# Retention attention and a SwiGLU block on one core: six instead of five pieces of a tick's vector work behind each plain down step

## The chip, the cores and the metric

The kernel runs on one core of a Trainium2 chip. The metric is the device time of one execution in microseconds (us); shorter is better. Engines are named as the profile names them: PE (matrix products), PEld (its weight loads), DVE (vector), ACT (scalar), POOL, and SP, which issues most of the transfers. Each engine runs its own instructions in the order in which they stand; semaphores tie them together.

## The reference

Attention with a decay in place of the softmax, for 8 batches x 8 heads x 576 positions x 64 columns, and behind it a SwiGLU block over 4608 tokens of 512 columns with 1536 hidden columns. All is float32.

```python
scores = scale * np.matmul(q, k.transpose(0, 1, 3, 2))
gamma = 1.0 - 2.0 ** (-5.0 - np.arange(H, dtype=np.float32))
Dmat = np.where(rel >= 0, gamma[:, None, None] ** rel[None, :, :], 0.0)   # rel = i - j
attn_out = np.matmul(scores * Dmat[None, :, :, :], v)
x = attn_out.transpose(0, 2, 1, 3).reshape(B * S, H * D)
g = x @ w_gate
silu = g * (1.0 / (1.0 + np.exp(-g)))
out = (silu * (x @ w_val) @ w_out)
```

## The kernel before

**Ticks.** The attention works on 32 pairs of heads (8 batches x 4 pairs). A pair passes through three ticks: in tick `t` the inputs of pair `t` are transposed, pair `t-1` gets its scores and its new states, and pair `t-2` gets its outputs. `tick(t)` first issues PE's part at once: `own_values(t-2)` (L519), `new_states(t-1)` (L529), `earlier_values(t-2)` (L540, L544), `scores(t-1)` (L552, L558). What the other engines do for the tick is put as closures ("pieces") into the list `pieces`, and `go_on(n)` runs the first `n` of them. For the ticks that matter here there are up to seven, in this order:

1. `copies` (L569): DVE copies one half of the new states out of PSUM, behind the last score of the tick;
2. `outputs` (L595, L609): DVE scales pair `t-2`'s outputs into x;
3. `own` (L565): DVE masks the scores of pair `t-1`;
4. `states` (L573 to L580): DVE chains the decayed states;
5. and 6. the two transposes of the inputs of pair `t` (L481);
7. `keys` (L496): DVE multiplies the keys of pair `t` (tile `kn`) with the decays, as one 128x256 and one 128x320 instruction. `new_states(t)`, which the next tick issues (L529), reads this `kn`.

**The stages.** (1) Pairs 0 to 9 with the weights' rounding and the first 512 tokens' up projection, `up0` (L690). (2) The plain down projection of these 512 tokens: twelve steps `m` = 0 to 11, each `down0(f)`, four matmuls over the four banks (L702), with ticks 10, 11, 12 and 13 behind steps 1, 3, 6 and 8. (3) Four tiles of 1024 tokens each, with fast matrix multiplication: 78 up steps (L919) and 26 down steps (L958) a tile, with sums of blocks before and after the products, on DVE and POOL (L726, L859, L888), and the remaining ticks spread among them.

**Inside stage 2.** A step issues, in this order: `down0(f)`; `go_on(5)`; if a tick is due, `tick(...)` and `go_on(1)`; then one group of `groups` and one of `last_groups`. A group prepares three of the 26 sums of blocks of `w_out` that stage 3 needs, and stores them in DRAM (`dn_ops`, L777). `groups` adds on POOL and stores by SP's queue, `last_groups` adds on DVE (L726, L721, L719) and stores by ACT's queue. From step 9 on DVE also makes the first sums of x for stage 3 (L726, `rest<-x_odd`). Every `tick` begins with `go_on(len(pieces))`, so a piece that is still waiting then is run ahead of it.

The order of PE, DVE, ACT, POOL and SP is the order in which the program issues (`tc.manual_schedule`); no scheduler moves an instruction. Ticks 10 and 11 have all seven pieces. Tick 12 has no transposes or keys, so four; tick 13 runs its pieces at once.

Of the kernel before, what the change touches and what calls it, by code (L numbers as in the profile page):

```python
# [154 lines left out]
def kernel(  # L155
# [101 lines left out]
    def needed(n):  # L257

        last = (min(starts[n] + TW, NT) - 1) // S
        return last * HP + HP - 1 + 3  # L260
# [375 lines left out]
    def tick(t, lo=HP, hi=NP, spread=False, then=None):  # L636
        go_on(len(pieces))
        if hi == HP:

            if lo <= t - 1 < hi:  # L640
                scores(t - 1, True)
                new_states(t - 1)
                for f in masked(t - 1):
                    f()
            if t == 3:
                split(0)
                rounding(0)
            if lo <= t - 2 < hi:
                own_values(t - 2)
                earlier_values(t - 2)  # L650
                to_x(t - 2)[0]()
            for f in transposes(t) if lo <= t < hi else ():
                f()
            return
        if lo <= t - 2 < hi:
            own_values(t - 2)
        if lo <= t - 1 < hi:
            new_states(t - 1)
        if lo <= t - 2 < hi:
            earlier_values(t - 2)  # L660
        if lo <= t - 1 < hi:
            scores(t - 1, t - 2 < lo)
        if lo <= t - 1 < hi and whole(t - 2) and not whole(t - 1):
            decay(slice(0, H), slice(0, H), half[1])
        copies, *masks = masked(t - 1) if lo <= t - 1 < hi else (lambda: None,)
        keys, *new = transposes(t) if lo <= t < hi else (lambda: None,)
        outputs = to_x(t - 2)[0] if lo <= t - 2 < hi else lambda: None
        if t - 2 >= 0 and light(t - 2):
            pieces.append(lambda: (copies(), keys(), outputs()))
        else:  # L670
            pieces.extend([lambda: (copies(), keys()), outputs])
        pieces.extend(masks)
        pieces.extend(new)
        if then:
            pieces.append(then)
        if not spread:
            go_on(len(pieces))

    def go_on(n):
        for _ in range(min(n, len(pieces))):  # L680
            pieces.pop(0)()
# [18 lines left out]
    def down0(f):  # L700
        for i, bank in enumerate(banks):
            nc.tensor.matmul(bank, hid0[f][:, ts(i, P)], w_dn[:, f // 4, f % 4].rearrange("p d x -> p (d x)"),  # L702
                             start=(f == down_order[0]), stop=(f == down_order[-1]))
# [171 lines left out]
    def x_sums(n, lo, hi, vector):  # L875
        for op in x_ops[lo:hi]:
            add(nc.vector if vector or op[0] == "nad" else nc.gpsimd, op, x_view(n))
# [14 lines left out]
    def first_sums(qd, lo, hi):  # L892

        engines = [nc.scalar, nc.gpsimd, nc.vector, nc.gpsimd]
        for op, eng in list(zip(up[0][5], engines, strict=True))[lo:hi]:
            if op[0] == "neg":
                nc.scalar.mul(out=up_view(qd)(int(op[1])), in_=up_view(qd)(int(op[2])), mul=-1.0)
            else:
                add(eng, op, up_view(qd))
        if hi == 4:  # L900
            w_sums(qd, 1)
# [132 lines left out]
    tick_at = {1: 10, 3: 11, 6: 12, 8: 13}  # L1034
    for m, f in enumerate(down_order):
        down0(f)
        go_on(5)
        if m in tick_at:
            tick(tick_at[m], HP, FIRST, tick_at[m] + 1 < needed(1))
            go_on(1)  # L1040
        if m == 8:
            first_sums(0, 0, 4)
        if m > 8:
            x_sums(1, 3 * (m - 9), min(3 * (m - 8), X_FIRST), True)
        if groups:
            groups.pop(0)[1]()
        if last_groups:
            last_groups.pop(0)()
# [58 lines left out]
```

## Time and profile before

| | |
|---|---|
| median of 4 runs | 1062.41 us (1061.71 to 1064.74) |
| the profiled execution | 1064.74 us |
| its span, first to last instruction | 1063.0 us |
| mean granted TensorE clock | 0.997 of full speed |
| PE busy | 1039.0 us, 98% of the span |
| DVE busy | 664.1 us, 62% |
| POOL busy | 389.1 us, 37% |
| ACT busy | 273.1 us, 26% |

The span leaves out 1.74 us of the profiled execution's time. The profiled execution is the longest of the four; the other three lie within 1.1 us of each other. Stage 2 lies between 127.9 and 185.9 us of the span, stage 3 follows to the end. Times with a decimal in the text below are microseconds from the span's start, where they are not durations.

### The profile page before, as it was taken

The page shows a single profiled execution, that of the slowest core. Times are in us where ns is not written, and L with a number is a line of the kernel's source. Part 1 is how long each engine was busy: PE and PEld are TensorE (multiplying, and loading weights), DVE is VectorE, ACT ScalarE, POOL GpSimd, SP SyncE. Part 2 cuts the span into 40 slices and gives each one's busy share as a digit, 9 for nine tenths or more (in the row PEclk, how much of TensorE's full clock was granted, in tenths as well). Part 3 has the DMA queues.
Part 4 walks back from the last instruction along what each step waited for, and adds up shares of the span by engine and source line. Part 5 has one row for each costly group of instructions (what it writes and reads, how often), then busy time and mean ns, then how long its engine had stood idle before and what let it go on. Part 6 is the DMA issues. An engine that isn't in the chain of part 4 may idle for free.

```text
span 1063.0 us, 21426 instructions
## 1 busy us (share of the span) xinstructions
PE 1039.0 (98%) x8448; PEld 852.3 (80%) x8448; DVE 664.1 (62%) x1094; ACT 273.1 (26%) x579; POOL 389.1 (37%) x338
## 2 busy tenths in 40 slices
PE   6999989999999999999999999999999999999998
PEld 5554555888787888888888888888888888888887
DVE  5568768896888668463557787526375554244644
ACT  4555400342433210332322112232220022222110
POOL 2002356656455206622224037512250384122505
PEclk9999999999999999999999999999999999999999
DMA  9898788646768869755766877554564455555553
GB/s 264 235 269 248 184 230 238 215 141 192 182 187 213 263 169 241 198 157 179 193 176 179 217 193 213 152 150 139 151 179 152 154 181 155 150 153 161 181 160 98
DMA packets 305083, 199.09 MB, mean 187 GB/s; under 512 B 219992, under 2 KB 248664, under 8 KB 304984
## 3 DMA queue, kind: packets, MB, share of 16 engines
q1 hardware_dynamic: 269528, 157.19, 54.3%
q10 hardware_dynamic: 35456, 40.54, 11.3%
q8 instruction: 67, 1.10, 0.4%
q14 instruction: 32, 0.26, 0.1%
HBM read 157.56 MB, written 40.11 MB: 186 GB/s over the span
## 4 chain that ended last, share of the span: by engine, by line
PE 84%; DVE 8%; DMA 3%; issue 2%; SPq 1%; POOL 1%; ACT 1%; ACTq 0%; DVEq 0%; POOLq 0%
PE bankC L919 11%; PE bankE L919 11%; PE bankB L919 11%; PE bankA L919 11%; PE bankA L958 6%; PE bankB L958 6%; PE bankE L958 6%; PE bankC L958 6%; DVE rest L859 3%; PE bankA L690 2%; PE outer L544 2%; PE bankC L690 2%; PE bankE L690 2%; PE bankB L690 2%; PE outer L519 2%
## 5 line engine op out<-in xcount | busy, mean ns | idle before, releaser
L859 POOL TENSOR_TENSOR rest<-rest 128x512 f32<-128x512 f32 x56 | 79.1, 1419 | 298.4 <-DVE rest L859 279.9
L934 ACT ACTIVATE io<-rest 128x256 f32<-128x256 f32 x180 | 75.0, 417 | 343.2 <-DVE rest L859 298.2
L919 PE MATMUL bankC<-rest,arena 128*128 128x256 f32 x544 | 129.2, 380 | 0.5 <-DVE rest L859 0.5
L919 PE MATMUL bankA<-rest,arena 128*128 128x256 f32 x544 | 129.0, 380 | 0.4 <-DVE rest L859 0.4
L726 POOL TENSOR_TENSOR arena<-arena 128x512 f32<-128x512 f32 (+1 forms) x72 | 113.7, 1592 | 32.4 <-DMA up<-arena 20.6
L919 PE MATMUL bankE<-rest,arena 128*128 128x256 f32 x512 | 121.4, 380 | 0.6 <-DVE rest L859 0.6
L919 PE MATMUL bankB<-rest,arena 128*128 128x256 f32 x512 | 121.5, 380 | 0.4 <-DVE rest L859 0.4
L919 PEld LDWEIGHTS bankA<-rest,arena 128*128 128x128 f32 x544 | 102.9, 190 | 15.8 <-issue 1.1
L919 PEld LDWEIGHTS bankC<-rest,arena 128*128 128x128 f32 x544 | 102.8, 190 | 15.6 <-issue 1.2
L941 POOL TENSOR_TENSOR arena<-rest,io 128x256 f32<-128x256 f32 x72 | 51.9, 727 | 166.7 <-ACT io L934 166.7
L919 PEld LDWEIGHTS bankE<-rest,arena 128*128 128x128 f32 x512 | 96.9, 190 | 14.6 <-DVE rest L859 1.0
L919 PEld LDWEIGHTS bankB<-rest,arena 128*128 128x128 f32 x512 | 96.9, 190 | 14.5 <-DVE rest L859 0.8
L726 POOL TENSOR_TENSOR rest<-rest 128x256 f32<-128x256 f32 (+1 forms) x66 | 65.8, 1017 | 102.3 <-DVE rest L416 59.7
L859 DVE TENSOR_TENSOR rest<-bankC,rest 128x512 f32<-128x512 f32 x72 | 48.9, 687 | 64.3 <-PE bankC L919 44.4
L859 DVE TENSOR_TENSOR rest<-bankB,rest 128x512 f32<-128x512 f32 x72 | 48.9, 687 | 64.1 <-PE bankB L919 46.1
L859 DVE TENSOR_TENSOR rest<-bankE,rest 128x512 f32<-128x512 f32 x72 | 48.9, 686 | 63.9 <-PE bankE L919 45.7
L859 DVE TENSOR_TENSOR rest<-bankA,rest 128x512 f32<-128x512 f32 x72 | 48.8, 686 | 63.5 <-PE bankA L919 46.2
L937 DVE SCALAR_TENSOR_TENSOR arena<-rest,io 128x256 f32<-128x256 f32 x84 | 57.3, 686 | 11.7 <-ACT io L934 11.7
L958 PE MATMUL bankA<-arena 128*128 128x256 f32 x252 | 58.0, 380 | 1.4 <-DVE arena L726 1.4
L958 PE MATMUL bankB<-arena 128*128 128x256 f32 x252 | 58.3, 381 | 0.0
L958 PE MATMUL bankC<-arena 128*128 128x256 f32 x252 | 58.1, 380 | 0.0
L958 PE MATMUL bankE<-arena 128*128 128x256 f32 x252 | 57.9, 379 | 0.0
(180 smaller groups left out, 1636.0 us busy)
## 6 DMA issues: line engine op xcount, KB each, us to landing
arena<-up SPq DMA_DIRECT2D x234, 256.0 KB, 2.6
arena<-dn SPq DMA_DIRECT2D x104, 384.0 KB, 3.3
up<-arena ACTq DMA_DIRECT2D x78, 256.0 KB, 2.6
out_dram<-rest SPq DMA_DIRECT2D x32, 256.0 KB, 3.6
qk<-in_q_dram SPq DMA_DIRECT2D x108, 72.0 KB, 2.6
qk<-in_k_dram SPq DMA_DIRECT2D x108, 72.0 KB, 2.3
dn<-rest SPq DMA_DIRECT2D x52, 128.0 KB, 2.3
rest<-in_moe_w_out_dram ACTq DMA_DIRECT2D x6, 1024.0 KB
```

Of the source, the lines that this page charges most:

```text
L519: m = nc.tensor.matmul(xo[half[hl ^ r * exchange(i)], c, r], s["v"][rows, at], ret[rows, r if whole(i) else hl, c], start=(c == 0), stop=( ...
L544: nc.tensor.matmul(xr[half[hl]] if c + 1 == NC else xo[half[hl ^ c % 2 * exchange(i)], c // 2, c % 2], state[half[hl], c, :], s["qT"][half ...
L690: nc.tensor.matmul(bank, w_up[:, f // 4, gv, f % 4, c // 2, (c % 2) * P : (c % 2 + 1) * P], xs[0][:, c, :], start=(c == 0), stop=(c == HP ...
L726: eng.tensor_tensor(out=dst, in0=srcs[0], in1=srcs[1], op=ALU.add if op[0] == "add" else ALU.subtract)
L859: eng.tensor_tensor(out=at(op[1]), in0=at(op[2]), in1=at(op[3]), op=ALU.add if op[0] == "add" else ALU.subtract)
L919: nc.tensor.matmul(b[:, gv * TB : (gv + 1) * TB], w[:, gv, ts(c, P)], rhs[:, c, :], start=(opens and gv == 0 and c == 0), stop=(c == 1), s ...
L934: nc.scalar.activation(out=s, in_=src[:, 0:TB], func=AF.Silu, scale=-1.0 if negative else 1.0)
L937: return lambda: nc.vector.scalar_tensor_tensor(out=dst, in0=src[:, TB : 2 * TB], scalar=-1.0, in1=s, op0=ALU.mult, op1=ALU.mult)
L941: nc.gpsimd.tensor_tensor(out=dst, in0=src[:, TB : 2 * TB], in1=s, op=ALU.mult)
L958: nc.tensor.matmul(b[:, m * TB : (m + 1) * TB], lhs[:, qd, ts(m, P)], w[:, qd], start=(opens and qd == 0 and m == 0), stop=(qd == NQ - 1), ...
```

## The change

One number changes: `go_on(5)` behind each `down0` becomes `go_on(6)`.

```diff
     for m, f in enumerate(down_order):
         down0(f)
-        go_on(5)
+        go_on(6)
         if m in tick_at:
             tick(tick_at[m], HP, FIRST, tick_at[m] + 1 < needed(1))
             go_on(1)
```

A tick with seven pieces runs one of them at its own step. Of the other six, the next step ran five and left the seventh, `keys`, to the step after that; now it runs all six. So `keys` of pair 10 moves from step 3 to step 2, and `keys` of pair 11 from step 5 to step 4, in each case ahead of the sums of that step's group on DVE (four instructions in step 2, three in step 4). The instructions of PE, ACT, POOL and SP stand in the order in which they stood.

## The prediction

> **What bounds the kernel now.** I read the page first, for who is busy and who is on the chain that ended last.
>
> ```profile
> PE 1039.0 (98%) x8448; PEld 852.3 (80%) x8448; DVE 664.1 (62%) x1094; ACT 273.1 (26%) x579; POOL 389.1 (37%) x338
> PE 84%; DVE 8%; DMA 3%; issue 2%; SPq 1%; POOL 1%; ACT 1%; ACTq 0%; DVEq 0%; POOLq 0%
> ```
>
> PE sets the time. So the change is worth what it takes from PE's idle time, or from the time that PE spends at a lower clock, and no more. The change lies in the plain down stage, 127.9 to 185.9, so I cut that stage and the beginning of the next into stretches (the table of windows: length, then busy time and count of PE, PEld, DVE, ACT, POOL, then the granted clock).
>
> ```profile
> 138.00:144.40 6.40, 6.40 (x16) 2.66 (x15) 6.29 (x19) 0.00 (x0) 2.35 (x3) 1.00 1.04 315
> 144.40:148.90 4.50, 1.40 (x37) 0.75 (x35) 4.41 (x6) 0.00 (x0) 4.10 (x6) 0.95 0.70 229
> 148.90:152.60 3.70, 3.70 (x103) 3.63 (x104) 0.00 (x0) 0.00 (x0) 2.81 (x4) 0.60 0.61 203
> 152.60:160.60 8.00, 8.00 (x19) 3.60 (x20) 7.89 (x19) 0.00 (x0) 7.83 (x12) 1.00 0.55 183
> 160.60:164.00 3.40, 3.17 (x40) 1.41 (x38) 3.37 (x6) 0.00 (x0) 3.31 (x5) 1.00 0.79 257
> 164.00:166.40 2.40, 2.37 (x103) 2.31 (x104) 1.72 (x3) 0.00 (x0) 2.23 (x4) 1.00 0.91 304
> 166.40:174.40 8.00, 7.91 (x58) 3.67 (x59) 7.83 (x18) 0.00 (x0) 6.76 (x8) 1.00 0.64 213
> ```
>
> Two rows stand out. From 144.4 to 148.9 PE is busy 1.40 of 4.50 us while DVE is busy 4.41; then, to 152.6, the two change places: DVE is busy 0.00 and PE works at a clock of 0.60. They wait for one another in turn. The timeline says for what: first PE, then DVE (start, duration, engine, line, count, and in brackets the idle time before it with its releaser).
>
> ```profile
> 144.77 0.69 PE L519 MATMUL outer<-ret,v 64*64 64x64 f32 x32
> 148.06 0.33 PE L529 MATMUL inner<-v,kn 64*64 64x64 f32 x2 [2.59 <-DVE kn L496]
> 148.90 1.02 PE L529 MATMUL inner<-v,kn 64*64 64x64 f32 x27 [0.51 <-DVE kn L496]
> ...
> 164.03 0.63 PE L529 MATMUL inner<-v,kn 64*64 64x64 f32 x27 [0.26 <-DVE kn L496]
> ```
>
> ```profile
> 143.64 0.73 DVE L481 STREAM_TRANSPOSE kT<-qk 128x576 f32<-128x576 f32 x1
> 144.30 2.97 DVE L726 TENSOR_TENSOR rest<-rest 128x256 f32<-128x256 f32 x4
> 147.20 1.64 DVE L496 TENSOR_SCALAR kn<-kn,tab 128x256 f32<-128x256 f32 x2
> 152.60 0.42 DVE L569 COPY even<-inner 128x256 f32<-128x256 f32 x1 [3.76 <-PE inner L558]
> ...
> 160.51 2.37 DVE L726 TENSOR_TENSOR rest<-rest 128x256 f32<-128x256 f32 x3
> 162.81 1.16 DVE L496 TENSOR_SCALAR kn<-kn,tab 128x256 f32<-128x256 f32 x2
> 163.89 0.94 DVE L721 SCALAR_TENSOR_TENSOR rest<-rest 128x256 f32<-128x256 f32 x1
> 164.76 0.94 DVE L726 TENSOR_TENSOR rest<-rest 128x256 f32<-128x256 f32 x1
> 166.39 0.42 DVE L569 COPY even<-inner 128x256 f32<-128x256 f32 x1 [0.68 <-PE inner L558]
> ```
>
> PE stands at tick 11's `new_states(10)` until DVE has scaled the keys, and DVE does four sums for the weight store first. Then DVE, with its sums done, waits 3.76 us for PE's tick. That is work in the wrong order on DVE, exactly where the change acts. At tick 12 the same is seen, but PE waits only 0.26 us.
>
> **The change, part by part.** No instruction is added or removed, and no transfer changes its place in its queue. Two pairs of L496 move up DVE's queue: one ahead of four L726 sums (step 2), one ahead of three (step 4). Ticks 12 and 13 have no sixth waiting piece and stay.
>
> *First place, DVE.* The second transpose ends at 144.37 (the next group's start in the chain of waits). The keys take 1.64 us as a pair, with POOL as busy then (its sums run from 144.51 to 148.66) as at 147.2. New end: 144.37 + 1.64 = 146.0. Cheapest would be two at the shortest L496, 0.40 each: 145.2. I keep 1.64. The four sums follow and end near 148.9, where the keys ended before.
>
> *First place, PE.* `own_values` ends at 145.46. The first keys are there at about 145.2, the second at 146.0, so PE idles some 0.6 us instead of 3.1. From its 27 L529 to the last score PE took 148.90 to 152.58 = 3.68 us; the same group in tick 12 took 164.03 to 166.33 = 2.30 us. The difference of 1.38 us is the clock: 0.60 in that stretch against 1.00. [...] the 0.26 us gap of tick 12 kept 1.00 in the trace. So PE ends the tick at 146.05 + 2.30 = 148.4, a gain of 4.2; were the clock still to drop, 149.7, a gain of 2.9.
>
> *DVE follows.* Its L569 starts when both PE (148.4) and its own sums (148.9) are done: 148.9 instead of 152.6, a gain of 3.7.
>
> *Second place.* From L569 to the end of the transposes DVE needs 152.60 to 160.58 = 7.98 us, so 156.9; keys by 158.0 to 158.5 (1.1 to 1.6 us). PE meanwhile has three down steps: twelve L702 at 0.86 = 10.3 us, so 148.4 + 10.3 + 0.6 (`own_values`) = 159.4. PE no longer waits for the keys; the 0.26 us, and some 0.2 us of the keys' second half, go too. PE ends tick 12 at about 161.7 (before 166.33, a gain of 4.6). DVE ends its three sums (2.37), L721 (0.94) and L726 (0.94) at 158.1 + 4.2 = 162.3; its L569 goes from 166.39 to 162.3, a gain of 4.1.
>
> *Third meeting.* In tick 13 PE's L544 needs the states of L580, which ended at 174.11 when PE arrived (174.07). DVE's are now ready at 170.0, PE is there at 169.7. DVE's 4.1 us decide, and PE carries them into its last three down steps: first L919 near 181.6 instead of 185.7.
>
> *Where I cost at nothing.* The four sums of step 2 end 1.6 us later, and so do their three stores on ACT's queue (L777). Behind these ACT has nothing but more stores until L897 at 176.78, which makes the first weight of the up stage; PE wants that at 181.6, so 4 us of cover are left. The stores share completion counters with SP's, so SP and POOL, which waits for free places, may slip by the same 1.6 us at most. POOL ends its sums at 172.05 and its next two stage-3 sums hang on DVE's L726 (176.36, now 172.3); the first weight it makes for PE there is used three up steps in, near 187. The transfer of pair 10's keys was issued at 133.51 and the median landing is 5.1 us, so about 139: it is there before 144.37, and so is pair 11's (issued at 133.73).
>
> [...] The last sums and the tick's vector work now run while POOL is still adding. In the trace a 128x256 L726 on DVE takes 0.42 us (174.03, POOL idle) and 0.94 (164.76, POOL busy). [...] Before, DVE left POOL alone for 3.7 us; that quiet time goes. By the rows the change moves about one such sum (174.03) under POOL, 0.5 us, and that one lies ahead of an idle time of 0.98 us (before L595), which covers it: 4.1 us stay. [...] But those four ran under POOL before as well (2.97 us for four that take 0.42 alone), so I take the rows.
>
> **Sum.** PE's whole loss around the keys is 2.59 + 0.51 + 0.26 us of idling and 1.38 us of clock = 4.74 us: the ceiling. Of it 4.1 us come out, set by DVE. Stage 3 is PE's: its waits from 190 to 345 come to 3.2 us in all, and loads, weights' sums and stores there hang on PE's and DVE's own progress, so an earlier start is passed on. Span 1063.0 - 4.1 = 1058.9; with the 1.74 us around it 1060.6 for an execution like the profiled one. That one is 2.33 above the median of the four runs; against the median I forecast 1062.41 - 4.1 = 1058.3.
>
> **The rivals.** *The gain is partly given back in the up stage* (1060.3 to 1058.9, 0.10). For it: from 185.7 to 202 DVE is busy 15.93 of 16.30 us, and PE waits for it 0.56 us at 202.07, so DVE has nothing to spare there. Against: all of DVE's work there begins earlier too. At one to three further sums under POOL (1.76 us for a 128x512 L726 at 190.38 against 0.69 alone, so 1.07 each) the gain is 1 to 3 us.
>
> *The wait only changes its name* (within 0.2%, 0.12). `new_states(10)` also waits for the loads of v and kn; were one of them the late one, keys scaled sooner would free nothing. v of pair 10 lands at 140.88 in the chain, which speaks against; a gain below 2 us would need three of the collisions above, or the low clock and one of them. Time: 1060.3 to 1062.4. That the change does nothing is excluded by the order of DVE's instructions.
>
> *Slower: collisions of DVE and POOL in the up stage* (0.08). From 185.7 to 226 POOL has 19 additions, some 1.3 us each, and DVE's two-input sums fall on them by chance of time. A shift of 4.1 us deals these meetings anew. At 1.07 us each, four more than now cancel the gain, and from six more on the kernel is over 0.2% slower: 1062.4 - 4.1 + 6 x 1.07 = 1064.7. For it: DVE is the pacemaker there. Against: POOL's additions wait for stores and for ACT, which hang on PE, so POOL moves along with DVE and the pattern should stay much the same.
>
> **How the numbers follow.** About 0.2%, 2.1 us, is what a measurement of this kernel can tell from no change. The likeliest case (gain of 3.5 to 4.8 us) has 0.68, the part given back that still leaves over 2.1 us 0.10, more than the ceiling by luck in stage 3 0.02: together 0.80 for faster. Within 0.2% 0.12, slower 0.08. The predicted time is the likeliest case's, 1058.3. The range goes from 1056.8 (the ceiling, 1057.7, and 0.9 for runs and stage 3) to 1061.4 (three collisions), which leaves out the slower case and the smaller half of the case of no difference.
>
> **What would show it.** Right: L496 directly behind the second L481 in both places; PE's wait before L529 down from 3.1 to about 0.6 us and none at tick 12; a granted clock near 1.00 through the stage; DVE's 3.76 us before L569 gone; first L919 near 181.6. Wrong: a wait of DVE on a transfer before L496; a clock still near 0.6; or a first L919 that is 4 us earlier with a span that is not, which would put the loss into stage 3.

## The result and the profile after

| | before | changed |
|---|---|---|
| median | 1065.27 us (64 runs, 1060.94 to 1071.52) | 1062.67 us (43 runs, 1058.66 to 1069.07) |
| ratio to before | | 0.9979, 95% interval 0.997 to 0.9988: 2.2 us less (1.3 to 3.2) |
| span of the profiled execution | 1063.0 us | 1060.0 us |
| mean granted clock | 0.997 | 0.999 |

The kernel is faster in this measurement, by about half of the forecast; two later series, below, show less. In time it lies 4.4 us above the 1058.3 us predicted and 1.3 us above the range. Two things are mixed there: the four runs shown before had a median of 1062.41, while 64 runs of the same kernel have 1065.27, so the level was 2.9 us low; and the gain is 2.2 us by the ratio, where 4.1 were forecast. Set on the level of the 64 runs, the same forecast would read 1061.2 us with a range from 1059.7 to 1064.3, and the measured 1062.67 would lie inside. So it is the level that put the time outside the range. The missing 1.9 us of gain are what has to be explained.

First the rows of the keys. The timeline of DVE in the changed kernel (start, duration, engine, line, count; in brackets the idle time before it with its releaser):

```profile
143.37 0.73 DVE L481 STREAM_TRANSPOSE kT<-qk 128x576 f32<-128x576 f32 x1
144.03 0.86 DVE L496 TENSOR_SCALAR kn<-kn,tab 128x256 f32<-128x256 f32 x2
144.81 2.48 DVE L726 TENSOR_TENSOR rest<-rest 128x256 f32<-128x256 f32 x4
147.84 0.42 DVE L569 COPY even<-inner 128x256 f32<-128x256 f32 x1 [0.55 <-PE inner L558]
...
161.05 0.42 DVE L569 COPY even<-inner 128x256 f32<-128x256 f32 x1 [1.99 <-PE inner L558]
```

L496 stands directly behind the transposes, and the pair took 0.86 us, not the 1.64 it took at its old place. DVE's idle time ahead of L569 fell from 3.76 to 0.55 us. The timeline of PE in the changed kernel, the two ticks and then the end of the down stage:

```profile
145.49 0.65 PE L529 MATMUL inner<-v,kn 64*64 64x64 f32 x32
...
158.70 0.65 PE L529 MATMUL inner<-v,kn 64*64 64x64 f32 x32
...
179.49 1.02 PE L702 MATMUL bankE<-rest,arena 128*128 128x512 f32 x2
182.16 1.99 PE L919 MATMUL bankA<-rest,arena 128*128 128x256 f32 x8 [1.66 <-ACT rest L708]
```

Both L529 groups run as 32 without a bracket: PE waits for no key of these two pairs at all. The windows of the changed kernel (length, then busy time and count of PE, PEld, DVE, ACT, POOL, then the granted clock, DMA share, GB/s) show that the clock stays up too:

```profile
144.40:148.90 4.50, 4.50 (x141) 3.32 (x140) 3.92 (x8) 0.00 (x0) 4.34 (x6) 1.00 0.77 254
148.90:152.60 3.70, 3.70 (x10) 1.60 (x9) 3.63 (x12) 0.00 (x0) 2.68 (x4) 1.00 0.77 252
174.40:185.70 11.30, 9.64 (x31) 5.56 (x30) 9.63 (x13) 2.23 (x4) 5.29 (x4) 1.00 0.89 228
```

PE is busy 4.50 of 4.50 us where it had been busy 1.40, and the stretch behind it runs at 1.00 in place of 0.60. So PE's last L702 ends at 179.49 + 1.02 = 180.51, against 185.87 before: 5.4 us earlier (5.6 us if both are counted from the stage's first L702), more than the 4.1 forecast. But the last window has 1.66 us of idling, and the last PE row above says why: the up stage's first product waits for ACT to copy bank A out (L708). That wait is new. ACT's instructions at this place are L897 and L887, which make weights of the up stage; L708, the copies of the down stage's banks; L710, the stores of these first 512 tokens' output; L922, the stores of the up stage's weight sums; and L856, the copies that free the up stage's banks for PE. Here ACT's timeline, before and then changed:

```profile
176.78 0.63 ACT L897 ACTIVATE arena<-arena 128x512 f32<-128x512 f32 x1 [47.43 <-DMA qk<-in_q_dram]
183.34 0.59 ACT L708 COPY rest<-bankA 128x512 f32<-128x512 f32 x1 [5.40 <-PE bankA L702]
187.69 0.58 ACT L856 COPY rest<-bankA 128x512 f32<-128x512 f32 x1 [2.91 <-PE bankA L919]
```

```profile
179.83 0.63 ACT L897 ACTIVATE arena<-arena 128x512 f32<-128x512 f32 x1 [50.27 <-DMA qk<-in_q_dram]
181.53 0.58 ACT L708 COPY rest<-bankA 128x512 f32<-128x512 f32 x1 [0.54 <-DMA dn<-rest]
...
187.60 0.58 ACT L856 COPY rest<-bankA 128x512 f32<-128x512 f32 x1 [5.00 <-DMA out_dram<-rest]
```

Before, both copies, L708 and L856, waited for PE (5.40 and 2.91 us): ACT had cover, which means that it could have come later by that much without PE's losing time. In the changed kernel both wait for transfers. L897 is 3.05 us *later* although PE is 5 us earlier, and L856 did not move at all (187.69 and 187.60). Something with a time of its own holds ACT. The queue of SP, before and then changed, shows what:

```profile
169.94 4.47 SPq L777 DMA_DIRECT2D dn<-rest  x7
174.84 2.09 SPq L293 DMA_DIRECT2D qk<-in_q_dram  x4
```

```profile
170.23 7.15 SPq L777 DMA_DIRECT2D dn<-rest  x9
177.81 2.07 SPq L293 DMA_DIRECT2D qk<-in_q_dram  x4
```

SP issues the loads of pair 12 (L293) behind the last stores of POOL's sums. POOL's sums now end at 175.04 instead of 172.05, so the loads start 2.97 us later. And the chain of waits of the changed kernel leads from there to L856 (start, duration, what):

```profile
180.07 3.14 DMA qk<-in_k_dram
183.21 0.02 issue
183.23 0.02 ACTq L710
...
183.77 3.81 DMA out_dram<-rest
187.58 0.01 issue
187.60 0.58 ACT rest L856
```

ACT's first output store (L710) waits for a *load* that SP issued. No data passes between the two. The semaphore numbers in the trace show what ties them. The transfers of SP (752) and of ACT (136) count their landings on the same eight completion counters, numbers 100 to 107, and 853 of these 888 transfers wait, just before they are issued, on the counter that they use themselves, which means for the landing of the one ahead of them on it. Three of ACT's four output stores stand behind loads of pair 12, the fourth behind ACT's last weight store (L777), which itself stands behind such a load. The first store of L922 stands behind another load of pair 12 (`kn`, landed at 187.15), ahead of L856 in ACT's queue; the second stands behind L710. L856, whose wait the two views above put down to the second output store (until 187.58), started at 187.60, right behind that first store of L922 (issued at 187.17, for 0.33 us). In this program a late load on SP (177.81 against 174.84) is therefore a late store on ACT, and with it a late bank copy.

### The profile page after: what moved, and what is told of

Read it like the earlier page. It is cut to its first block, busy times and chain, and to the rows that moved or that the text cites. A ratio compares the mean times of both kernels' runs of the same rounds, so it can differ in the third digit from the quotient of the medians.

```text
span 1060.0 us, 21426 instructions
## 1 busy us (share of the span) xinstructions
PE 1037.6 (98%) x8448; PEld 850.8 (80%) x8448; DVE 661.8 (62%) x1094; ACT 273.2 (26%) x579; POOL 389.8 (37%) x338
## 3 DMA queue, kind: packets, MB, share of 16 engines
q1 hardware_dynamic: 269528, 157.19, 54.7%
## 4 chain that ended last, share of the span: by engine, by line
PE 82%; DVE 5%; POOL 4%; DMA 3%; issue 2%; ACT 1%; SPq 0%; ACTq 0%; DVEq 0%; POOLq 0%
PE bankC L919 11%; PE bankE L919 11%; PE bankB L919 11%; PE bankA L919 11%; PE bankA L958 6%; PE bankB L958 6%; PE bankE L958 6%; PE bankC L958 6%; DVE rest L859 3%; PE bankA L690 2%; PE bankC L690 2%; PE bankB L690 2%; PE bankE L690 2%; POOL rest L726 2%; PE outer L544 2%
## 5 line engine op out<-in xcount | busy, mean ns | idle before, releaser
L919 PE MATMUL bankA<-rest,arena 128*128 128x256 f32 x544 | 129.1, 380 | 2.4 <-ACT rest L708 1.7
L919 PE MATMUL bankC<-rest,arena 128*128 128x256 f32 x544 | 129.2, 380 | 0.8 <-DVE rest L859 0.5
L726 POOL TENSOR_TENSOR arena<-arena 128x512 f32<-128x512 f32 (+1 forms) x72 | 113.7, 1591 | 27.4 <-DMA up<-arena 19.2
L919 PE MATMUL bankE<-rest,arena 128*128 128x256 f32 x512 | 121.5, 380 | 0.5 <-DVE rest L859 0.5
L919 PE MATMUL bankB<-rest,arena 128*128 128x256 f32 x512 | 121.4, 380 | 0.4 <-DVE rest L859 0.4
L919 PEld LDWEIGHTS bankA<-rest,arena 128*128 128x128 f32 x544 | 102.8, 190 | 18.3 <-ACT rest L708 2.5
L919 PEld LDWEIGHTS bankC<-rest,arena 128*128 128x128 f32 x544 | 102.8, 190 | 15.8 <-issue 1.2
L919 PEld LDWEIGHTS bankE<-rest,arena 128*128 128x128 f32 x512 | 96.8, 190 | 14.6 <-DVE rest L859 0.9
L919 PEld LDWEIGHTS bankB<-rest,arena 128*128 128x128 f32 x512 | 96.9, 190 | 14.4 <-DVE rest L859 0.8
L726 POOL TENSOR_TENSOR rest<-rest 128x256 f32<-128x256 f32 (+1 forms) x66 | 66.8, 1033 | 101.5 <-DVE rest L416 58.3
L958 PE MATMUL bankA<-arena 128*128 128x256 f32 x252 | 58.0, 380 | 1.4 <-DVE arena L726 1.4
L958 PE MATMUL bankB<-arena 128*128 128x256 f32 x252 | 58.3, 381 | 0.0
L958 PE MATMUL bankC<-arena 128*128 128x256 f32 x252 | 58.1, 380 | 0.0
L958 PE MATMUL bankE<-arena 128*128 128x256 f32 x252 | 57.9, 379 | 0.0
```

The source lines that it names most:

```text
L726: eng.tensor_tensor(out=dst, in0=srcs[0], in1=srcs[1], op=ALU.add if op[0] == "add" else ALU.subtract)
L919: nc.tensor.matmul(b[:, gv * TB : (gv + 1) * TB], w[:, gv, ts(c, P)], rhs[:, c, :], start=(opens and gv == 0 and c == 0), stop=(c == 1), s ...
L958: nc.tensor.matmul(b[:, m * TB : (m + 1) * TB], lhs[:, qd, ts(m, P)], w[:, qd], start=(opens and qd == 0 and m == 0), stop=(qd == NQ - 1), ...
```

## The experiments

The question was why 5.4 us at the end of the down stage became 2 us in the whole. The theory: POOL's chain and the shared counters hold ACT, and ACT holds PE where the stages meet. The rivals: the ACT queue is just too long; the gain is lost to DVE and POOL colliding in the up stage, as the prediction had it; the two moved pairs are of unequal worth. As runs of one kernel differ by several us and the down stage itself begins anywhere from 126.1 to 132.4 in the profiles, the ratios decide, and of each profile the stretches from the stage's first L702 are read. These are seen in one execution each, and not always in a typical one: the profiles of r_after and e_pair10 are of the slowest of their 14 runs, that of e_before_relief is of the fastest.

| kernel | ratio to before, 95% interval | runs | first L702 to first L919, us | first L702 to first ACT L856 | first L702 to first L958 |
|---|---|---|---|---|---|
| before | | | 57.8 | 59.8 | 211.6 |
| changed | 0.9979 (0.997 to 0.9988) | 43 | 54.0 | 59.5 | 208.7 |
| r_after, changed again | 0.9993 (0.998 to 1.0007) | 14 | 52.5 | 61.0 | 209.4 |
| r_after2, changed again | 0.9994 (0.9977 to 1.0012) | 14 | 54.3 | 61.8 | 211.0 |
| e_store_tail | 0.9993 (0.9976 to 1.001) | 14 | 54.6 | 61.6 | 210.8 |
| e_after_relief | 0.9964 (0.9953 to 0.9974) | 21 | 52.2 | 57.2 | 206.4 |
| e_before_relief | 0.9996 (0.9979 to 1.0012) | 14 | 55.1 | 57.1 | 208.6 |
| e_out_sp | 0.9967 (0.9954 to 0.998) | 22 | 52.2 | 54.2 | 207.1 |
| r_out_sp2, e_out_sp again | 0.9964 (0.9948 to 0.998) | 10 | 53.1 | 55.2 | 207.4 |
| e_before_out_sp | 0.999 (0.9971 to 1.0008) | 14 | 57.6 | 59.6 | 210.4 |
| e_out_sp_io | 0.9977 (0.9966 to 0.9988) | 17 | 52.7 | 54.7 | 207.5 |
| e_pair10 | 0.9999 (0.998 to 1.0018) | 14 | 54.0 | 60.3 | 209.2 |
| e_pair11 | 1.0001 (0.9983 to 1.0019) | 14 | 57.5 | 59.5 | 210.6 |
| e_out_sp_relief | 0.9939 (0.9915 to 0.9963) | 6 | 52.2 | 54.2 | 205.9 |

**The changed kernel again** (r_after, and later r_after2).

> The changed kernel again, as the measure for the three others of this group. Both theories: about 2.2 us below the kernel before (ratio near 0.998), with a wait of PE of about 1.7 us for ACT's L708 ahead of the first L919 near 182.2.

> The changed kernel a third time, on one chip with the next: ratio to the kernel before 0.998 to 0.9995. Theory 1 wants it slower than the next kernel by 1 to 3 us, theory 2 (DVE and POOL collide in the up stage) equal to it.

Measured 0.9993 and 0.9994, the first short of its expectation. So the gain of this kernel came out as 2.2, 0.7 and 0.6 us; the three intervals overlap between 0.998 and 0.9988, and in the two later ones no gain can be told from none. In both new profiles ACT is late again, but not at the same place. In the timeline of PE in r_after, and in the windows of the same run, the loss has moved one step on:

```profile
182.89 1.99 PE L919 MATMUL bankA<-rest,arena 128*128 128x256 f32 x8 [0.17 <-ACT rest L708]
192.61 3.23 PE L919 MATMUL bankA<-rest,arena 128*128 128x256 f32 x8 [2.54 <-ACT rest L856]
```

```profile
185.70:202.00 16.30, 13.76 (x57) 11.51 (x56) 11.58 (x16) 4.88 (x10) 5.97 (x5) 0.90 0.95 261
```

PE got past L708 with 0.17 us, then waited 2.54 us for the late L856 (it came 61.0 us after the stage's start), and the granted clock was 0.90 in that stretch: just behind the wait eight products took 3.23 us, where the eight after the 0.17 us wait took 1.99. In r_after2 the two waits were 1.72 and 1.58 us. So ACT's lateness takes back 1.7 us to over 3, at L708, at L856, or at both. That this alone makes the three ratios differ is not shown; the runs of this kernel spread over 6.5 to 10.4 us in each series.

**Is it ACT's queue?** e_store_tail puts the last eight stores of `last_groups` on SP's queue, so that ACT's is empty earlier:

```diff
-                queue.dma_start(out=dn_ops[i]...
+                (nc.sync if k >= ends[18] else queue).dma_start(out=dn_ops[i]...
```

> The changed kernel, with the last eight of DVE's stores (L777) issued by SP's queue instead of ACT's. Theory 1 (ACT's last stores, which wait behind SP's stores of POOL's sums, hold up L897, L887 and the L708 copies that free the banks): L897 well before 175, PE's wait ahead of the first L919 down from 1.66 us to under 0.6, the kernel 1 to 1.7 us faster than the changed one. Theory 2 (the missing 2 us are lost in the up stage, by collisions of DVE and POOL): the boundary may move, the time stays within 0.5 us of the changed kernel.

Measured 0.9993: missed. The timeline of ACT and then that of PE in this kernel:

```profile
180.46 0.59 ACT L708 COPY rest<-bankA 128x512 f32<-128x512 f32 x1 [15.57 <-DMA dn<-rest]
```

```profile
181.10 1.99 PE L919 MATMUL bankA<-rest,arena 128*128 128x256 f32 x8 [1.74 <-ACT rest L708]
```

ACT had stood idle for 15.57 us and still copied late, since a weight store had not landed; its L856 then waited 6.51 us, put down to a load of pair 12. So it does not help that ACT's queue is empty early. (The edit puts eight more stores ahead of SP's loads of pair 12, which began at 180.46 and not at 177.81, so its time shows both effects at once.) That part of the theory fell; the transfers' landing stayed.

**Is it POOL's chain?** The relief kernels leave out the last eleven additions of POOL's weight sums (the sums they store are not complete), once in the changed kernel and once in the kernel before:

```diff
-                add(eng, e[1], view, new)
+                qd == 1 and k > ends[11] or add(eng, e[1], view, new)
```

> The changed kernel without eleven of POOL's last additions for the second column group in the plain down stage (their sums are left out, the stores stay). Theory 1 (POOL's sums set when the stores and with them ACT's L708 come): POOL is through some 8 us sooner, near 167, PE reaches the first L919 near 180.7 without waiting, 1.5 us faster than the changed kernel at least. Theory 2 (the loss is in the up stage): no more than 0.5 us faster than the changed kernel.

> The kernel before, without the same eleven POOL additions (their sums are left out). Theory 1: there POOL's chain was hidden behind PE, so within 0.7 us of the kernel before; what falls is some DVE time from collisions. A general benefit of less POOL work (theory 2's reading of the run with the changed kernel) would show here as well, 1.5 us or more.

Measured 0.9964 in the changed kernel, 0.9996 in the kernel before. The same work taken from POOL is worth 3.1 us in the changed kernel (0.9964 against 0.9993 for r_after in the same series; the intervals do not overlap) and nothing that can be measured in the kernel before. The timeline of ACT in e_after_relief:

```profile
181.57 0.58 ACT L708 COPY rest<-bankA 128x512 f32<-128x512 f32 x1 [1.40 <-PE bankA L702]
...
188.93 0.58 ACT L856 COPY rest<-bankA 128x512 f32<-128x512 f32 x1 [5.91 <-DMA out_dram<-rest]
```

L708 waits for PE again. L856's wait is still put down to an output store (5.91 us), but at 57.2 us of the stage it is 2.3 us earlier than in the changed kernel, and PE did not wait for it. The shorter chain brings the transfers forward; it does not cut the tie. In the kernel before, POOL's chain was covered; in the changed kernel it is no longer. (The shorter stretches of e_before_relief in the table come from its one profiled execution, in which PE waited 1.30 us for the first keys where the kernel before had waited 2.59; the additions left out lie behind that place.)

**Is it the tie of ACT's stores to SP's loads?** POOL's sums are needed, so a real repair has to cut the tie. e_out_sp lets SP issue the four output stores, ahead of the loads of pair 12; e_before_out_sp is the same edit on the kernel before; e_out_sp_io also copies banks A and B into `io`, so that L708 has no place that a weight store still reads.

```diff
-            nc.scalar.dma_start(out=out[i * P : (i + 1) * P, :], ...
+            nc.sync.dma_start(out=out[i * P : (i + 1) * P, :], ...
```

> The changed kernel, with the four stores of the first 512 tokens' output (L710) issued by SP's queue ahead of the load of pair 12, instead of by ACT's. Theory 1 (the gain is lost at the boundary to the up stage, where ACT's stores L710 and L922, and with them the L856 that frees a bank, wait for completion counters shared with the load of pair 12, which SP issues only behind POOL's last stores): ACT's first L856 no longer waits for a transfer but for PE, near 184 to 186 instead of 187.6 to 191.4, no PE wait for L856, the kernel 1 to 2 us faster than the changed kernel (ratio to the kernel before 0.995 to 0.998). Theory 2 (lost to collisions of DVE and POOL in the up stage): no change against the changed kernel.

> The kernel before with the same L710 on SP's queue. Theory 1: there ACT's L856 waited for PE and not for a transfer, so nothing is won: within 0.1% of the kernel before. If it gains as much as the same edit on the changed kernel, the boundary was lossy before the change too and theory 1 explains none of the missing gain.

> As the first of this group, and two of the four bank copies (L708 on ACT) go into the tile io, which no store of w_out's sums is still reading. Theory 1: L708 of banks A and B no longer waits for the landing of such a store, so PE's wait ahead of the first L919 (1.66 us) shrinks to what ACT's own last stores take, under 1 us; 0.3 to 1 us faster than without this edit. Theory 2: no change.

Measured 0.9967, 0.999 and 0.9977. The edit does more than free L710. The loads of pair 12, now behind the output stores, start at 182.94 in e_out_sp and not at 177.81, and the counters are dealt out anew: ACT's last weight store and the first L922 no longer stand behind a load of pair 12 (L922 went out at 178.86, not at 187.17). The timelines of PE and of ACT in e_out_sp:

```profile
180.28 1.89 PE L919 MATMUL bankA<-rest,arena 128*128 128x256 f32 x8
```

```profile
178.70 0.59 ACT L708 COPY rest<-bankA 128x512 f32<-128x512 f32 x1 [0.73 <-DMA dn<-rest]
182.27 0.59 ACT L856 COPY rest<-bankA 128x512 f32<-128x512 f32 x1 [2.50 <-PE bankA L919]
```

PE enters the up stage without a wait, and L856 waits for PE as it did before the change, 5.4 us earlier than it ran then. The edit alone is worth nothing that can be measured on the kernel before, though its interval reaches down to 0.9971. e_out_sp_io brought none of the 0.3 to 1 us that were expected; with the tie cut, L708's places cost nothing that can be measured.

Run again as r_out_sp2, e_out_sp gave the same:

> The changed kernel with L710 issued by SP, again. Theory 1: ratio to the kernel before 0.995 to 0.998, and 0.997 to 0.999 of the changed kernel beside it. If it falls back to the changed kernel's time, the earlier 0.9967 was chance and the boundary explains nothing.

Measured 0.9964, median 1062.11 us, beside 1064.98 us of the changed kernel in the same series. The timeline of ACT in r_out_sp2:

```profile
183.39 0.59 ACT L856 COPY rest<-bankA 128x512 f32<-128x512 f32 x1 [1.65 <-PE bankA L919]
```

In this profile POOL's sums ended at 175.33, as late as in the changed kernel (175.04), and L856 still waited for PE, at 55.2 us of the stage. So most of the cost is not POOL's end as such, but what hangs on it. By the ratios this version, `go_on(6)` with the output stores on SP, is the fastest full computation that was tried: 0.9967 and 0.9964, against 0.9979, 0.9993 and 0.9994 of the changed kernel, with intervals that overlap. What is not separated is which part of the edit does it: the counters that ACT's stores wait on, or the loads of pair 12 that no longer run beside them. The chain above speaks for the counters: ACT's first output store and L856 come right after such landings. In the kernel before, the same edit, which puts the loads behind the output stores there too, brought nothing measurable (0.999).

**Which of the two moved pairs?** e_pair10 moves only the keys of pair 10, e_pair11 only those of pair 11:

```diff
-        go_on(6)
+        go_on(6 if m == 2 else 5)     # e_pair10;  m == 4 in e_pair11
```

> One half of the change: only the keys of pair 10 move up (step 2), those of pair 11 stay behind the three sums of step 4's group. Both theories: nearly the whole effect, since PE waited 3.1 us for pair 10's keys and 0.26 us for pair 11's: PE ends the plain down stage some 4.5 us earlier than before, and the time is that of the changed kernel within 0.1%.

> The other half: only the keys of pair 11 move up. PE waited 0.26 us for them, so at most 0.5 us; within 0.1% of the kernel before. PE still waits some 3 us for pair 10's keys at tick 11.

Measured 0.9999 and 1.0001: neither alone does anything that can be measured. For pair 10 nearly the whole effect was expected. For pair 11 that is no surprise, 0.26 us was all it had on PE. In the profile of e_pair10 the wait for pair 10's keys is gone, tick 12 waits 0.58 and 0.44 us for those of pair 11, and the down stage is as short as in the changed kernel (54.0 us); then L856 comes at 60.3 us behind a wait of 6.04 us, put down to the output stores. That fits the same hold, but with intervals of 0.2% it is a fit and no proof.

**Is there more behind POOL?** e_out_sp_relief has both the output stores on SP and the eleven additions left out.

> L710 on SP, and eleven of POOL's last additions in the plain down stage left out (their sums are left out, the stores stay). Theory 1: with the boundary already free of waits there is nothing left for POOL's relief to bring: within 0.1% of the kernel with L710 on SP alone. If it is 1 us or more faster, POOL's chain still holds something up there.

Measured 0.9939, against 0.9964 for r_out_sp2 beside it, where no difference was expected; with six runs the intervals overlap (0.9915 to 0.9963 and 0.9948 to 0.998). The profiles show a part of it. With the tie cut, PE waits 0.67 us (e_out_sp) and 0.62 us (r_out_sp2) for one of POOL's sums early in the up stage; in e_out_sp_relief this wait is gone, and the first L958 comes 1.2 and 1.5 us sooner. So POOL seems to hold a little more; what the rest of the 2.7 us between the two ratios is stays open.

## Why the prediction was wrong in size

- *What bounds the kernel, and the ceiling.* The reading was right: PE's two waits for keys, the clock of 0.60 behind the first, and DVE's idle time ahead of L569 were one knot, and it is gone. 57.8 us of down stage became 54.0. The ceiling of 4.74 us was too low. From its first L519 to the next L702 tick 11 took 2.71 us (144.98 to 147.69) in place of 7.71, and tick 12 2.71 in place of 3.28: 5.57 us together.
- *The price of the keys.* Put at 1.64 us for the pair with a lower bound of 0.80; it was 0.86 for pair 10 and 0.74 for pair 11, though POOL was busy then. PE's rest of 0.6 us of waiting was not there (so the estimate that the clock stays at 1.00 behind such a gap was not put to the test), and PE came through 5.4 us earlier and not 4.1. This was an error in the cautious direction.
- *"Where I cost at nothing": the term that was mis-sized.* The text gave ACT 4 us of cover, from L897 at 176.78 to PE's need at 181.6, and let SP and POOL slip "by the same 1.6 us at most". Measured, SP's loads of pair 12 slipped by 2.97 us and L897 by 3.05. POOL's share of this is visible. Its first sum behind the long wait started 0.85 us later (142.81 against 141.96), one more wait of 1.19 us for a store came at 153.54, and from that first sum to the last POOL was busy 29.46 us in place of 28.13, 1.33 us more. Whether DVE's work beside it caused this 1.33 us is not shown by a run of its own; the prediction weighed such collisions, but for DVE's loss only (0.42 us for a 128x256 L726 with POOL idle, 0.94 us for one with POOL busy).
- *The cover was read only to its first consumer.* L897 itself, ending at 180.46, was about in time for PE, whose last L702 ended at 180.51. What came late was behind it in the same queue: L708, then L710, L922 and L856, held by transfers. L856 did not move at all. The text looked at none of these, though all four stand in ACT's timeline of before, two of them with 5.40 and 2.91 us of waiting for PE: that, and no more, was the cover.
- *"An earlier start is passed on."* This step failed. The prediction rested it on loads, sums and stores that "hang on PE's and DVE's own progress". The loads of pair 12 hang on POOL's last stores, and ACT's stores and bank copies hang on these loads. Counted from the stage's first L702, PE was 5.6 us ahead at its last L702, 3.8 at the first L919 and 3.0 at the first L958 (2.2 and 0.7 in the profiles of r_after and r_after2). With the tie cut it was 4.5 and 4.2 us ahead of the kernel before at the first L958, and 3.5 to 3.8 us by the ratios. Like with like, e_out_sp against e_before_out_sp, the keys' new place is worth 3.3 us to the first L958 and 2.4 us by the ratios (0.9967 and 0.999, intervals that overlap). So the tie explains a good part of the gap to the forecast of 4.1; whether all of it, these intervals do not tell.
- *The rivals.* "Partly given back in the up stage" by collisions was the nearest in time, but not by its mechanism: in the profiled execution of the changed kernel 1.66 of the 2.6 us lost between the last L702 and the first L958 are a wait for L708 where the stages meet, and from 185.7 to 202 DVE was busy 15.25 us, not more than the 15.93 before. "The wait only changes its name" came near as well: PE's wait for keys was replaced by waits for ACT's copies, and 0.9993 and 0.9994 lie within that case's 0.2%; but the loads of v and kn, on which the prediction hung it, were not late. The slower case did not come.
- *The level.* The median of four runs was taken as the base, though the profiled execution was 2.33 us above it. 64 runs say that the profiled execution (1064.74) was the typical one. The four runs were low, by chance as far as the record tells, and this term alone put the time above the range; the step at the seam halved the gain.

## What to carry to other kernels

When the bounding engine is made to arrive earlier, everything that used to wait for it must be able to come earlier too: list each release that it needs at the next seam of stages, down to the last bank copy, and ask of each whether it hangs on that engine or on a chain with its own time. A wait for the bounding engine in a helper's row (here ACT's 5.40 and 2.91 us) is the cover; in the changed kernel it was used up, and that helper's transfers decided (0.54 and 5.00 us of waiting for them at the same two places). Here it helped, by the ratios (0.9967 and 0.9964 against 0.9979, 0.9993 and 0.9994), that stores which release what the bounding engine needs no longer stood, by queue or by completion counter, behind loads that wait for another engine.

## What the runs showed of the hardware

- The queues of SP and ACT, which share eight completion counters in this program, were not independent: an output store of ACT waited for a load of SP with which it shares no data (L710 went on at 183.23, behind `qk<-in_k_dram`, landed at 183.21). Four stores issued by another engine were worth 1.3 to 3.2 us, by the ratios of e_out_sp and r_out_sp2 against the three of the changed kernel.
- The two L496 instructions took 0.86 and 0.74 us at their new places and 1.64 and 1.16 at the old ones, with POOL busy in each case. So a duration read at one place of DVE's order was no fixed price at another.
- Behind waits of PE of 2.59 and 0.51 us the granted clock was 0.60 over 3.7 us in the kernel before (148.9 to 152.6). With a wait of 2.54 us it was 0.90 over 16.3 us in r_after (185.7 to 202), and the eight L919 products behind the wait took 3.23 us. With a wait of 1.66 us it was 1.00 in the changed kernel (174.4 to 185.7), and the eight products behind the wait took 1.99 us; behind the waits of 1.72 and 1.58 us in r_after2 they took 1.99 and 1.96 us.
- The beginning of the down stage differs by up to 6.3 us between profiled executions (126.1 to 132.4), more than the whole change is worth; only stretches within a profile, and ratios over many runs, could be compared.
